# Polynomial-sketch attention with an ELU layer: two more query units through the 64-feature exchange, and the last half group's query products put beside others

## The chip, the core and the metric

The kernel runs on one core of one Trainium2 chip. The metric is the device time in microseconds. The engines named below are TensorE (PE in the profile, PEld for its weight loads), VectorE (DVE), ScalarE (ACT), GpSimd (POOL) and SyncE (SP), which issues nearly all DMAs.

## The reference

```python
# q, k, v: (4, 4, 1088, 32); S1, S2: (8, 32)
def phi(x):                                   # 8 x 8 = 64 features
    a = np.einsum('rd,bhsd->bhsr', S1, x)
    b = np.einsum('rd,bhsd->bhsr', S2, x)
    return np.einsum('bhsi,bhsj->bhsij', a, b).reshape(*x.shape[:-1], r * r)
q_p, k_p = phi(q), phi(k)
kv = np.einsum('bhsf,bhsd->bhfd', k_p, v)
z = np.sum(k_p, axis=2)
num = np.einsum('bhsf,bhfd->bhsd', q_p, kv)
den = np.einsum('bhsf,bhf->bhs', q_p, z)[..., None] + 1e-06
x = (num / den) -> (B, S, H, D) -> (4352, 128)
h = x @ w_in                                  # w_in: 128 x 2048
g = np.where(h > 0, h, np.exp(np.minimum(h, 0)) - 1)
out = g @ w_out                               # w_out: 2048 x 128
```

S1, S2 and the two weight matrices come as 64-bit floats and are rounded to 32 bits on the chip (`RA`, `RB`, `RC` round a pair of weight blocks); all products are in 32 bits.

## The kernel before

**Tiling.** A half tile is 64 query positions of one batch with all four heads (128 rows of head and dimension). Each batch has 17. `half_tile(g, k)` puts the first 16 of every batch into groups 0 to 7, eight to a group (512 output tokens), two groups to a batch; group 8, the last half group, is the 17th half tile of each of the four batches (256 tokens). `NQ` is 9.

**The steps.** The second stage runs per group over 8 pairs of 128-column blocks of `w_in` (`cp`). A step is one (group, `cp`): `mm1` (h products, L267), the elu on ACT (`e`, L928 and L930) and DVE (`gg`, L936), on POOL the sums for a seven-product scheme (`sums7`, L811 to L814, tiles `tt`), and on PE the second product of the step two before (`mm2`, `mm2_blocks` L827 or `mm2_seven` L851). The list `steps` has groups 0 and 1 interleaved in steps 0 to 15, then group 2 in steps 16 to 23, group 3 in 24 to 31, and so on to group 7 in 56 to 63. A loop over n from 5 to 63 writes the order by hand; after it the last half group runs in 20 short rounds.

**What is put into steps.** `at(n, f)` puts a call right behind `mm1` of step n, `mid(n, f)` behind the elu of the first half, `late(n, f)` behind that of the second, ahead of the step's second product. Every engine takes its instructions in this order.

**Keys.** For batches 1 to 3: `KF_late` (features by PE), `KF_late_out` (DVE), `KO_a` and `KO_b` (the 64 products per position; ACT and DVE, or POOL by `KO`), `KA` (PE: kv and the z sums), `sums_out` (`ZC`, and `KT_out`, which sends kv through DRAM, tile `kvd`, into the layouts that the queries need), `turn` and `turned` (the weights `SWs` that hold z for a batch's denominators).

**Queries.** A unit is one or two groups: unit 2 is group 2, unit 3 is group 3, unit 4 is groups 4 and 5, unit 6 is groups 6 and 7, unit 8 is the last half group. For a unit: `q1`, called its keys below (PE: a, b and the z share of every position, 32x32 tiles, L579), `q1_out` (DVE transposes, L592 or L602), `q2_den` (four DVE instructions: denominators, and a divided by them), `q2_a` (a copy to PSUM on ACT, tile `qa`), `q2_half` (DVE: 64 features per position, L714), `q4` (DVE transpose, features into rows), `q5`, its sums for x (PE), `q5_out` (ACT copies into `xg`, from which `mm1` reads).

`q4` has two forms. Without an exchange (units 2, 3, 4) the features stay in 32 rows in two halves `f`, and `q5` (L741) makes each product twice over 32 features in 32x32 tiles. With one (`pairs`, units 6 and 8) eight DMAs on SP for each half i of the unit, 64 KB each (L732, tile `qpF` to `raw`), bring two halves of the features into 64 rows, and `q5_pairs` (L753) makes each product once in 64x32 tiles, from the layout `kv2` (tile `kvp`) instead of `kvs`.

**The stops.** `queries(g5, g1, n)` makes the sums of one unit and the keys of another between `mm1` and the second product of a step; it writes into the two `h` tiles of the next step (of four) and two `aux` tiles. Its calls stand at steps 12 (keys 2), 15 (sums 2), 22 (sums 3, keys 4), 30 (sums 4, keys 6), 46 (sums 6, keys 8) and 62 (sums 8).

**SP's order.** It issues the loads, then `kvd`, `kvs` and `kvp`, the exchanges and the outputs (16 DMAs for each of groups 1 to 7, `fin_seven_b`, L899) strictly in the order above; the load of q of batch 3 waits until batch 1's q is transposed.

Of the kernel before, what the change touches and what calls it, by code (L numbers as in the profile page):

```python
# [29 lines left out]
def kernel(  # L30
# [306 lines left out]
    kvS = const.tile([P, H, D], F32, name="kvS")  # L337
    pairs = (6, 8)
    pair_b = [g // 2 for g in pairs if g < 8]
    kvs = {b: const.tile([P, H, 2, D], F32, name=f"kvs{b}") for b in (1, 2)}  # L340
    kv2 = {b: const.tile([P, H, D], F32, name=f"kvp{b}") for b in range(B)}
# [121 lines left out]
    def KT_out(b):  # L463

        kt = work.tile([P, 2 * D], F32, name="kvt", tag="kvt")
        nc.vector.transpose(kt[:], kv_ps[b][:, :R * R])
        nc.sync.dma_start(kvd[b], kt[:])
        src = kvd[b].rearrange("(h p) x -> p h x", h=H)
        for w in range(4 if b in kvs else 0):
            nc.sync.dma_start(kvs[b][32 * w:32 * w + 32].rearrange("p h f d -> p h (f d)"), src)  # L470
        for u in (0, 1) if b in pair_b else (b // 2,):
            for f in range(2):
                r = slice(64 * u + 32 * f, 64 * u + 32 * f + 32)
                nc.sync.dma_start(kv2[b][r], src[:, :, D * f:D * f + D])
# [38 lines left out]
    qn = [min(8, NH - 8 * g) // 2 for g in range(NQ)]  # L513
    abw, ans, qp, qpT, xg, xps = {}, {}, {}, {}, {}, {}
    pws = [const.tile([P, H * 8, R + 1], F32, name=f"pw{i}") for i in range(2)]
# [45 lines left out]

    units = {g: ([g, g + 1] if 4 <= g < NQ - 1 else [g]) for g in [2, 3] + list(range(4, NQ, 2))}
    un = {g: sum(qn[x] for x in gr) for g, gr in units.items()}
# [5 lines left out]

    def q1(g, ps, o, opened):  # L570
        for w in range(4):
            b, t, n = quarter_of(g, w)
            m, qs = 64 * n, qE[:, b:b + 1, :] if g == NQ - 1 and b < 2 else qT[b][:, t:t + n, :]
            qs = qs.rearrange("p t s -> p (t s)")
            if g == 2:
                m, qs = 2 * m, _ap(qs, [[8 * 64, 2], [1, m]])
            for r in range(4):
                rows = slice(32 * r, 32 * r + 32)
                nc.tensor.matmul(ps[r][32 * w:32 * w + 32, o:o + m], SWs[rows, b].rearrange("p x r -> p (x r)"),  # L579
                                 qs[rows], start=not opened, stop=True, skip_group_check=True,  # L580
                                 tile_position=(32 * r, 32 * w))
        abw[g] = ps, o

    def q1_out_two(rs):
        if 3 not in abw:
            abw[2, 3] = abw[2][0]
            t = work.tile([P, 2, 4 * H, 4 * R], F32, name="abw2", tag="abw2", bufs=1)
            abw[2], abw[3] = t[:, 0], t[:, 1]
            abw[2, 0] = t
        n = 4 * H // 4  # L590
        for r in rs:
            nc.vector.transpose(abw[2, 0][:, :, n * r:n * r + n, :].rearrange("p g m y -> p g (m y)"),  # L592
                                abw[2, 3][r][:, :64 * n].rearrange("p (g m) -> p g m", g=2))

    def q1_out(g):
        (ps, o), n = abw[g], un[g]
        pair = n > 4
        abw[g] = work.tile([P, H * n if pair else H * 4, 4 * R], F32, name="abw", tag="abwp" if pair else "abw",
                           bufs=1 if pair else 2)
        m = H * n // len(ps)  # L600
        for r in range(len(ps)):
            nc.vector.transpose(abw[g][:, m * r:m * r + m, :].rearrange("p m y -> p (m y)"),  # L602
                                ps[r][:, o:o + 32 * m])
# [82 lines left out]
    def q5_early_out(g, w):  # L686
# [6 lines left out]
        else:  # L693
# [3 lines left out]
    exch = [raw_2[:, c].bitcast(F32).rearrange("p (e m a) w -> p e m (a w)", e=2, a=16) if wide else  # L697
            const.tile([P, 2, 4 * H, 32], F32, name=f"qpE{c}")[:] for c in range(2)]

    def heads(g):  # L700
        return 2 if un[g] > 4 else H
# [15 lines left out]
    def q4(g, i=0):  # L717

        m = heads(g) * un[g]
        if g not in pairs:  # L720
            qpT[g, i] = work.tile([P, 4 * H, 2, 32], F32, name="qpT", tag="qpT", bufs=2)
            nc.vector.transpose(qpT[g, i][:, :m].rearrange("p m f s -> p (m f s)"),
                                qp.pop((g, i))[:, :m].rearrange("p m i j -> p (m i j)"))
            return
        t = work.tile([P, 2, 4 * H, 32], F32, name="qpF", tag="qpT", bufs=2)
        nc.vector.transpose(t[:, :, :m].rearrange("p f m s -> p m f s"),
                            qp.pop((g, i))[:, :m].rearrange("p m (f i) j -> p m f (i j)", f=2))
        to = qpT[g, i] = exch[(i + (g > 3)) % 2]
        for e in range(2):
            for u in range(0, 4, 2):  # L730
                for f in range(2):
                    nc.sync.dma_start(to[32 * (u + f):32 * (u + f) + 32, e, :m], t[32 * (u + e):32 * (u + e) + 32, f, :m])  # L732

    def q5(g, ps, f):
        m4 = un[g]
        for r in range(4):
            i, o = divmod(m4 * r, heads(g) * un[g])
            for w in range(4):
                b, t, n = quarter_of(g, w)
                rows = slice(32 * w, 32 * w + 32)  # L740
                nc.tensor.matmul(ps[w][32 * r:32 * r + 32, :64 * n], kvs[b][rows, r, f, :],  # L741
                                 qpT[g, i][rows, o:o + 2 * n, f, :], start=(f == 0), stop=(f == 1),
                                 skip_group_check=True, tile_position=(32 * w, 32 * r))
        xps[g] = ps

    def q5_pairs(g, ps):
        for e in range(2):
            for r in range(4):
                i, o = divmod(un[g] * r, heads(g) * un[g])
                for w in (e, e + 2):  # L750
                    b, t, n = quarter_of(g, w)
                    u = slice(64 * (w // 2), 64 * (w // 2) + 64)
                    nc.tensor.matmul(ps[w][32 * r:32 * r + 32, :64 * n], kv2[b][u, r, :],  # L753
                                     qpT[g, i][u, e, o:o + 2 * n, :], skip_group_check=True,
                                     tile_position=(u.start, 32 * r))
        xps[g] = ps

    def q5_out(g, i=0):

        n = 32 * un[g]  # L760
        ps = xps[g] if len(units[g]) == 1 else xps[g][2 * i:2 * i + 2]
        x = xg[g + i] = work.tile([P, 512], F32, name="xg", tag="xg", bufs=3)
        for w in range(len(ps)):
            nc.scalar.copy(x[:, n * w:n * w + n], ps[w][:, :n])

    def queries(g5, g1, n):

        hs[steps[n]] = [psum.tile([P, 512], F32, name="h", tag="h", bufs=4) for c in range(2)]
        ps = hs[steps[n]] + [psum.tile([P, 512], F32, name="qps", tag="aux") for _ in range(2)]
        if g5 in pairs:  # L770
            q5_pairs(g5, ps)
        elif g5 is not None:
            q5(g5, ps, 0)
        if g1 is not None:
            q1(g1, ps, 256 if g5 is not None else 0, g5 is not None)
        if g5 is not None and g5 not in pairs:
            q5(g5, ps, 1)

# [402 lines left out]

    for n, i in ((5, 7), (7, 8), (9, 9), (10, 10)):
        late(n, RA, i)
        late(n, RB, i)
        mid(n + 1, RC, i)

    late(14, keep_last, 1)
    zls = {}
# [13 lines left out]
    for b, (n_t, n_f, n_o, n_a, n_z) in enumerate(  # L1202
            ((4, 6, (7, 9), 10, 11), (14, 16, (17, 18), 19, 20), (15, 16, (23, 24), 27, 28)), 1):
        if b > 1:
# [16 lines left out]
        at(n_z, turned, b)  # L1221
    late(10, transp, qT, "q", 1, 0, NT)
    at(19, transp, qT, "q", 2, 0, NT)
    late(24, transp, qT, "q", 3, 0, NT)

    for n, g, nx in ((12, None, 2), (15, 2, None), (22, 3, 4), (30, 4, 6), (46, 6, 8), (62, 8, None)):
        at(n, queries, g, nx, n + 1)
        if g is not None:
            mid(n, q5_out, g)
        if nx == 2:  # L1230
            at(n, weights7, slice(NP - 2, NP))
            at(n, q1_out_two, (0, 1))
            mid(n, q1_out_two, (2, 3))
        elif nx is not None:
            mid(n, q1_out, nx)
        if g is not None and len(units[g]) > 1:
            late(n, q5_out, g, 1)
    late(12, q2_den, 2)
    late(13, q2_half, 2, 0)
    at(14, q4, 2)  # L1240
    mid(15, q2_den, 3)
    late(19, q2_a, 3, 0)
    late(19, q2_half, 3, 0)
    late(20, q4, 3)
    late(22, q2_den, 4)
    for n, g, i in ((25, 4, 0), (26, 4, 1), (32, 6, 0), (35, 6, 1)):
# [9 lines left out]
    late(38, q4, 6, 1)  # L1256
    late(51, q2_den, 8)
    late(51, q2_half, 8, 0)
    late(52, q4, 8)

# [102 lines left out]
```

## Time and profile before

| | |
|---|---|
| median of 3 runs | 261.6 us (260.96 to 262.27) |
| the profiled execution | 261.49 us, span 259.7 us |
| PE busy | 254.4 us, 98% |
| DVE, ACT, POOL busy | 178.9, 184.9, 167.7 us |
| products of h (L267) in the chain that ended last | 45% of the span |
| exchange DMAs (qpF), 64 KB and 32 KB | 24, landing 2.0 us after issue (median) |
| output DMAs of groups 0 to 7, 16 KB each or 32 KB | 120 |

The page is one execution on the chip. Its chain of waits follows the work that ended last back in time. A line of the chain or of a timeline is: start, duration, engine and what, line, how often. A matmul in 32 bits is recorded as two. `SPq` rows are SP's DMA issues: start, and how long the run of issues held the queue.

### The profile page before, as it was taken

The numbers are of one execution on the slowest core, as the hardware profiler recorded it, in microseconds if no ns is written. First come the engines' busy times: TensorE is split into PE (matmuls) and PEld (weight loads), VectorE is DVE, ScalarE is ACT, GpSimd is POOL, SyncE is SP. The second block draws the span as 40 slices with busy tenths as digits, with TensorE's granted clock in tenths as the row PEclk, the third lists the DMA queues.
The fourth block names the chain that finished last, engine by engine and source line by source line (L and its number), as shares of the span: only waits on it lengthen the run. The fifth ranks groups of instructions, "written<-read, shape, count | busy, mean of one in ns | idle before, by whom it ended". The sixth has DMA issues, their size and how long they took to land.

```text
span 259.7 us, 9773 instructions
## 1 busy us (share of the span) xinstructions
PE 254.4 (98%) x4115; PEld 157.8 (61%) x4115; DVE 178.9 (69%) x343; ACT 184.9 (71%) x362; POOL 167.7 (65%) x213
## 2 busy tenths in 40 slices
PE   8999999999999999999999999999999999999994
PEld 7742333533346667676666666665666666668993
DVE  6989776896988958997567576743466746544651
ACT  2699878756568677776687777775877777777792
POOL 4634214234279996788688798888688888887310
PEclk9999999999999999999999999999999999999999
DMA  5999990012011211012000204220001110110021
GB/s 171 261 311 294 299 247 23 0 26 89 20 22 25 33 27 23 5 17 35 15 0 3 36 17 105 51 33 10 4 4 28 31 27 3 28 16 3 3 30 33
DMA packets 30379, 15.61 MB, mean 60 GB/s; under 512 B 22496, under 2 KB 28000, under 8 KB 30336
## 3 DMA queue, kind: packets, MB, share of 16 engines
q1 hardware_dynamic: 29904, 14.63, 23.6%
q8 instruction: 32, 0.52, 0.8%
q10 hardware_dynamic: 368, 0.30, 0.3%
q14 instruction: 11, 0.09, 0.1%
q0 software_dynamic: 64, 0.07, 0.1%
HBM read 11.31 MB, written 2.36 MB: 53 GB/s over the span
## 4 chain that ended last, share of the span: by engine, by line
PE 96%; DVE 2%; ACT 1%; issue 0%; DVEq 0%
PE h L267 45%; PE pb L851 17%; PE pa L851 13%; PE o L267 6%; PE pb L827 4%; PE ol L267 3%; PE idle L275 1%; PE kv L458 1%; PE h L741 1%; PE h L579 1%; PE abp L354 1%; DVE kp L427 1%; PE h L753 1%; PE kfps L376 0%; PE qps L741 0%; PE qtp L657 0%
## 5 line engine op out<-in xcount | busy, mean ns | idle before, releaser
L267 PE MATMUL h<-xg,W 128*32 128x512 f32 (+3 forms) x904 | 131.0, 540 | 0.0
L936 DVE SCALAR_TENSOR_TENSOR gg<-e,h 128x512 f32<-128x512 f32 x128 | 87.0, 684 | 59.3 <-ACT e L930 56.4
L928 ACT ACTIVATE e<-h 128x512 f32<-128x512 f32 x128 | 75.3, 590 | 48.6 <-PE h L267 48.5
L811 POOL TENSOR_TENSOR tt<-gg 128x512 f32<-128x512 f32 x50 | 64.3, 1286 | 30.1 <-DVE gg L936 26.3
L930 ACT ACTIVATE e<-e 128x512 f32<-128x512 f32 x128 | 80.6, 631 | 3.7
L267 PEld LDWEIGHTS h<-xg,W 128*32 128x32 f32 (+1 forms) x904 | 42.7, 122 | 42.8 <-issue 34.0
L814 POOL TENSOR_TENSOR tt<-gg,tt 128x256 f32<-128x256 f32 x50 | 37.0, 740 | 3.9
L813 POOL TENSOR_TENSOR tt<-tt,gg 128x256 f32<-128x256 f32 x50 | 36.8, 736 | 3.9
L851 PEld LDWEIGHTS pa<-gg,W 128*64 128x64 f32 (+1 forms) x496 | 23.7, 126 | 22.4 <-issue 22.2
L851 PE MATMUL pa<-gg,W 128*64 128x128 f32 (+1 forms) x496 | 30.6, 274 | 0.0
L142 POOL TENSOR_TENSOR W<-W,raw 128x256 uint32<-128x256 uint32 (+2 forms) x12 | 11.8, 987 | 29.1 <-DVE W L119 28.0
L851 PE MATMUL pb<-tt,SS 128*64 128x128 f32 (+1 forms) x480 | 29.6, 273 | 0.0
L851 PEld LDWEIGHTS pb<-tt,SS 128*64 128x64 f32 (+1 forms) x480 | 22.8, 126 | 0.0
L851 PE MATMUL pa<-tt,SS 128*32 128x128 f32 (+1 forms) x288 | 21.2, 273 | 0.0
L851 PE MATMUL pb<-gg,SS 128*64 128x128 f32 (+1 forms) x256 | 19.9, 273 | 0.0
L851 PE MATMUL pb<-tt,W 128*64 128x128 f32 (+1 forms) x256 | 19.9, 273 | 0.0
L267 PE MATMUL o<-gg,W 128*32 128x512 f32 x128 | 15.5, 595 | 0.0
L851 PEld LDWEIGHTS pa<-tt,SS 128*32 128x32 f32 (+1 forms) x288 | 13.7, 124 | 0.0
L851 PEld LDWEIGHTS pb<-gg,SS 128*64 128x64 f32 (+1 forms) x256 | 12.8, 125 | 0.0
L851 PEld LDWEIGHTS pb<-tt,W 128*64 128x64 f32 (+1 forms) x256 | 12.8, 125 | 0.0
L827 PE MATMUL pb<-gg,W 128*32 128x256 f32 x192 | 11.5, 379 | 0.0
L989 DVE SCALAR_TENSOR_TENSOR gg<-e,h 128x256 f32<-128x256 f32 x16 | 6.6, 418 | 6.4 <-PE h L267 3.2
(169 smaller groups left out, 261.5 us busy)
## 6 DMA issues: line engine op xcount, KB each, us to landing
raw<-in_moe_w_in_dram SPq DMA_DIRECT2D x8, 256.0 KB, 5.9
raw<-in_moe_w_out_dram SPq DMA_DIRECT2D x8, 256.0 KB, 4.6
out_dram<-ob SPq DMA_DIRECT2D x112, 16.0 KB, 1.5
hd_k<-in_k_dram SPq DMA_DIRECT2D x3, 544.0 KB, 9.9
hd_q<-in_q_dram SPq DMA_DIRECT2D x3, 544.0 KB, 11.3
v<-in_v_dram SPq DMA_DIRECT2D x4, 288.0 KB, 10.0
v<-in_v_dram SPq DMA_DIRECT2D x4, 256.0 KB, 10.5
raw<-qpF SPq DMA_DIRECT2D x16, 64.0 KB, 2.0
```

The costliest lines, as they stand in the source:

```text
L142: nc.gpsimd.tensor_tensor(dst.bitcast(U32), dst.bitcast(U32), words(raw)[0], op=ADD)
L267: nc.tensor.matmul(dst[c:c + tile], lhs[:, c:c + tile], rhs, skip_group_check=True, tile_position=(0, c), **kw)
L275: nc.tensor.matmul(idle[c:c + tile, :cols], ones[:, :tile], ones[:, :cols], skip_group_check=True, tile_position=(0, c))
L811: nc.gpsimd.tensor_tensor(_ap(t[:, 0], [[4 * P, 2], [P, 2], [1, P]]), _ap(gs[g, cp][:, 0, P:], [[4 * P, 2]] + us), _ap(gs[g, cp][:, 0], [[ ...
L813: nc.gpsimd.tensor_tensor(t[:, 1], t[:, 2], b11, op=ADD)
L814: nc.gpsimd.tensor_tensor(t[:, 3], b21, t[:, 1], op=SUB)
L827: nc.tensor.matmul(acc[1][0][r:r + width[0], 256 * hi:256 * hi + 256], lhs[:, w:w + width[0]], gg[:, c, 256 * u:256 * u + 256], start=(fir ...
L851: nc.tensor.matmul(bank[r:r + width[0], P * col:P * col + P], lhs[:, w:w + width[0]], rhs[:, u], start=(first and i in ((0,) if g == 1 els ...
L928: nc.scalar.activation(e, hs[g, cp][c][:, :n], RELU, scale=-1.0)
L930: nc.scalar.activation(e, e, EXP, scale=-1.0)
L936: nc.vector.scalar_tensor_tensor(gs[g, cp][:, c, :n], es[g, cp][:, c, :n], -1.0, hs[g, cp][c][:, :n], op0=ADD, op1=MAX)
L989: nc.vector.scalar_tensor_tensor(gs["last", k // 2][:, k % 2, :2 * P], es["last", k // 2][:, k % 2, :2 * P], -1.0, hs["last", k][:, :2 * P ...
```

## The change

- Unit 2 is groups 2 and 3 together, as 4 and 6 are; unit 3 is gone. All units from 2 up take the exchange and `q5_pairs`; `q5`, `kvs` and their DMAs are gone. `kv2` of batches 1 to 3 is filled for both row halves (four DMAs each), of batch 0 for one (two).
- `queries` takes lists. Stops: step 11 (keys 2), 15 (sums 2), 25 (keys 4 and 8), 30 (sums 4, keys 6), 46 (sums 6 and 8). A second unit of a stop writes 256 columns further on in the same banks.
- Unit 8's tile `qpE2` and x tile `xgl` are its own.
- The key work of batch 1 is one step earlier; of batch 3, the products move from steps 23 and 24 to 20 and 21, `KA` from 26 and 27 to 22 and 23, `turn` from 28 to 24. Two of the weight roundings, and the transposes of q for batches 1 and 3, are one or two steps earlier.

```diff
-    pairs = (6, 8)
-    pair_b = [g // 2 for g in pairs if g < 8]
-    kvs = {b: const.tile([P, H, 2, D], F32, name=f"kvs{b}") for b in (1, 2)}
...
-        for w in range(4 if b in kvs else 0):
-            nc.sync.dma_start(kvs[b][32 * w:32 * w + 32].rearrange("p h f d -> p (h f d)"), src)
-        for u in (0, 1) if b in pair_b else (b // 2,):
+        for u in (0, 1) if b else (0,):
...
-    units = {g: ([g, g + 1] if 4 <= g < NQ - 1 else [g]) for g in [2, 3] + list(range(4, NQ, 2))}
+    units = {g: ([g, g + 1] if g < NQ - 1 else [g]) for g in range(2, NQ, 2)}
...
+    exch += [const.tile([P, 2, 2 * H, 32], F32, name="qpE2")[:]]
...
     def q4(g, i=0):
...
-        if g not in pairs:
-            qpT[g, i] = work.tile([P, 4 * H, 2, 32], F32, name="qpT", tag="qpT", bufs=2)
-            nc.vector.transpose(qpT[g, i][:, :m].rearrange("p m f s -> p (m f s)"),
-                                qp.pop((g, i))[:, :m].rearrange("p m i j -> p (m i j)"))
-            return
...
-        to = qpT[g, i] = exch[(i + (g > 3)) % 2]
+        to = qpT[g, i] = exch[i if g < NQ - 1 else 2]
...
-    def queries(g5, g1, n):
+    def queries(g5s, g1s, n):
...
-        if g5 in pairs:
-            q5_pairs(g5, ps)
-        elif g5 is not None:
-            q5(g5, ps, 0)
-        if g1 is not None:
-            q1(g1, ps, 256 if g5 is not None else 0, g5 is not None)
-        if g5 is not None and g5 not in pairs:
-            q5(g5, ps, 1)
+        sums = [(g, 256 * i) for i, g in enumerate(g5s)]
+        keys = [(g, 256 * i) for i, g in enumerate(g1s, len(g5s))]
+        for g, c in sums:
+            q5_pairs(g, ps, c)
+        for g, c in keys:
+            q1(g, ps, c)
...
-    for n, i in ((5, 7), (7, 8), (9, 9), (10, 10)):
+    for n, i in ((5, 7), (7, 8), (8, 9), (9, 10)):
...
-            ((4, 6, (7, 9), 10, 11), (14, 16, (17, 18), 19, 20), (15, 16, (23, 24), 27, 28)), 1):
+            ((4, 5, (6, 8), 9, 10), (14, 16, (17, 18), 19, 20), (15, 16, (20, 21), 23, 24)), 1):
...
-    for n, g, nx in ((12, None, 2), (15, 2, None), (22, 3, 4), (30, 4, 6), (46, 6, 8), (62, 8, None)):
-        at(n, queries, g, nx, n + 1)
+    for n, g5s, g1s in ((11, (), (2,)), (15, (2,), ()), (25, (), (4, NQ - 1)), (30, (4,), (6,)), (46, (6, NQ - 1), ())):
+        at(n, queries, g5s, g1s, n + 1)
...
-    late(12, q2_den, 2)
-    late(13, q2_half, 2, 0)
-    at(14, q4, 2)
-    mid(15, q2_den, 3)
-    late(19, q2_a, 3, 0)
-    late(19, q2_half, 3, 0)
-    late(20, q4, 3)
-    late(22, q2_den, 4)
+    late(11, q2_den, 2)
+    mid(12, q2_half, 2, 0)
+    late(12, q4, 2, 0)
+    mid(13, q2_half, 2, 1)
+    late(13, q4, 2, 1)
+    late(25, q2_den, 4)
     for n, g, i in ((25, 4, 0), (26, 4, 1), (32, 6, 0), (35, 6, 1)):
         late(n, q2_a, g, i)
     at(26, q2_half, 4, 0)
     late(26, q2_half, 4, 1)
     late(27, q4, 4, 0)
     late(28, q4, 4, 1)
...
-    late(51, q2_den, 8)
-    late(51, q2_half, 8, 0)
-    late(52, q4, 8)
+    late(40, q2_den, 8)
+    late(41, q2_half, 8, 0)
+    late(42, q4, 8)
```

More of the change, by code (lines that the diff above doesn't have):

```diff
@@ L468, in KT_out @@
         src = kvd[b].rearrange("(h p) x -> p h x", h=H)
-        for w in range(4 if b in kvs else 0):
-            nc.sync.dma_start(kvs[b][32 * w:32 * w + 32].rearrange("p h f d -> p h (f d)"), src)
-        for u in (0, 1) if b in pair_b else (b // 2,):
+        for u in (0, 1) if b else (0,):
             for f in range(2):
@@ L513 @@
     qn = [min(8, NH - 8 * g) // 2 for g in range(NQ)]
-    abw, ans, qp, qpT, xg, xps = {}, {}, {}, {}, {}, {}
+    abw, ans, qp, qpT, xg, xps, qps = {}, {}, {}, {}, {}, {}, {}
     pws = [const.tile([P, H * 8, R + 1], F32, name=f"pw{i}") for i in range(2)]
@@ L568, in quarter_of, with q1 @@
         return (*half_tile(g + n * w // 8, n * w % 8), n)
-    def q1(g, ps, o, opened):
+    def q1(g, ps, o):
         for w in range(4):
@@ L574, in q1 @@
             qs = qs.rearrange("p t s -> p (t s)")
-            if g == 2:
-                m, qs = 2 * m, _ap(qs, [[8 * 64, 2], [1, m]])
             for r in range(4):
@@ L579, in q1, with q1_out @@
                 nc.tensor.matmul(ps[r][32 * w:32 * w + 32, o:o + m], SWs[rows, b].rearrange("p x r -> p (x r)"),
-                                 qs[rows], start=not opened, stop=True, skip_group_check=True,
+                                 qs[rows], skip_group_check=True,
                                  tile_position=(32 * r, 32 * w))
         abw[g] = ps, o
[L584 to L596, printed above, removed]
-        pair = n > 4
-        abw[g] = work.tile([P, H * n if pair else H * 4, 4 * R], F32, name="abw", tag="abwp" if pair else "abw",
-                           bufs=1 if pair else 2)
+    def q1_out(g, rs=None):
+        n = un[g]
+        pair = n > 4
+        if g not in qps:
+            qps[g] = abw[g]
+            abw[g] = work.tile([P, H * n if pair else H * 4, 4 * R], F32, name="abw", tag="abwp" if pair else "abw",
+                               bufs=1)
+        ps, o = qps[g]
         m = H * n // len(ps)
-        for r in range(len(ps)):
+        for r in range(len(ps)) if rs is None else rs:
             nc.vector.transpose(abw[g][:, m * r:m * r + m, :].rearrange("p m y -> p (m y)"),
@@ L732, in q4, with q5_pairs @@
                     nc.sync.dma_start(to[32 * (u + f):32 * (u + f) + 32, e, :m], t[32 * (u + e):32 * (u + e) + 32, f, :m])
[L734 to L746, printed above, removed]
+    def q5_pairs(g, ps, c=0):
         for e in range(2):
@@ L752, in q5_pairs @@
                     u = slice(64 * (w // 2), 64 * (w // 2) + 64)
-                    nc.tensor.matmul(ps[w][32 * r:32 * r + 32, :64 * n], kv2[b][u, r, :],
+                    nc.tensor.matmul(ps[w][32 * r:32 * r + 32, c:c + 64 * n], kv2[b][u, r, :],
                                      qpT[g, i][u, e, o:o + 2 * n, :], skip_group_check=True,
                                      tile_position=(u.start, 32 * r))
-        xps[g] = ps
+        xps[g] = [p[:, c:] for p in ps]
     def q5_out(g, i=0):
@@ L761, in q5_out @@
         ps = xps[g] if len(units[g]) == 1 else xps[g][2 * i:2 * i + 2]
-        x = xg[g + i] = work.tile([P, 512], F32, name="xg", tag="xg", bufs=3)
+        if g < NQ - 1:
+            x = xg[g + i] = work.tile([P, 512], F32, name="xg", tag="xg", bufs=3)
+        else:
+            x = xg[g] = work.tile([P, 2 * P], F32, name="xgl", tag="xgl", bufs=1)
         for w in range(len(ps)):
             nc.scalar.copy(x[:, n * w:n * w + n], ps[w][:, :n])
-    def queries(g5, g1, n):
+    def queries(g5s, g1s, n):
         hs[steps[n]] = [psum.tile([P, 512], F32, name="h", tag="h", bufs=4) for c in range(2)]
         ps = hs[steps[n]] + [psum.tile([P, 512], F32, name="qps", tag="aux") for _ in range(2)]
-        if g5 in pairs:
-            q5_pairs(g5, ps)
-        elif g5 is not None:
-            q5(g5, ps, 0)
-        if g1 is not None:
-            q1(g1, ps, 256 if g5 is not None else 0, g5 is not None)
-        if g5 is not None and g5 not in pairs:
-            q5(g5, ps, 1)
+        sums = [(g, 256 * i) for i, g in enumerate(g5s)]
[4 more added lines that the diff above has]
+            q1(g, ps, c)
     hs, es, gs, ops = {}, {}, {}, {}
@@ L1180, in late @@
         extra.setdefault((n, 1), []).append((f, *a))
-    for n, i in ((5, 7), (7, 8), (9, 9), (10, 10)):
[L1183 to L1187, printed above, removed]
     zls = {}
@@ L1221 @@
         at(n_z, turned, b)
-    late(10, transp, qT, "q", 1, 0, NT)
+    for n, i in ((5, 7), (7, 8), (8, 9), (9, 10)):
+        late(n, RA, i)
+        late(n, RB, i)
+        mid(n + 1, RC, i)
+    late(9, transp, qT, "q", 1, 0, NT)
+    late(12, keep_last, 1)
     at(19, transp, qT, "q", 2, 0, NT)
-    late(24, transp, qT, "q", 3, 0, NT)
-    for n, g, nx in ((12, None, 2), (15, 2, None), (22, 3, 4), (30, 4, 6), (46, 6, 8), (62, 8, None)):
-        at(n, queries, g, nx, n + 1)
-        if g is not None:
+    late(22, transp, qT, "q", 3, 0, NT)
+    for n, g5s, g1s in ((11, (), (2,)), (15, (2,), ()), (25, (), (4, NQ - 1)), (30, (4,), (6,)), (46, (6, NQ - 1), ())):
+        at(n, queries, g5s, g1s, n + 1)
+        for g in g5s:
             mid(n, q5_out, g)
[L1230 to L1237, printed above, removed]
-    late(12, q2_den, 2)
-    late(13, q2_half, 2, 0)
-    at(14, q4, 2)
-    mid(15, q2_den, 3)
-    late(19, q2_a, 3, 0)
-    late(19, q2_half, 3, 0)
-    late(20, q4, 3)
-    late(22, q2_den, 4)
+        for g in g1s:
+            if g == 2:
+                at(n, q1_out, g, (0, 1))
+                mid(n, q1_out, g, (2, 3))
+            else:
+                mid(n, q1_out, g)
+        for g in g5s:
+            if len(units[g]) > 1:
+                late(n, q5_out, g, 1)
+    at(12, weights7, slice(NP - 2, NP))
+    late(11, q2_den, 2)
[4 more added lines that the diff above has]
+    late(25, q2_den, 4)
     for n, g, i in ((25, 4, 0), (26, 4, 1), (32, 6, 0), (35, 6, 1)):
```

## Prediction

> **What bounds the kernel now.** I read the page's busy line first, then the chain of waits in order of time, then the timelines of SP, VectorE (DVE), ScalarE (ACT) and GpSimd (POOL) around the changed steps.
>
> ```profile
> PE 254.4 (98%) x4115; PEld 157.8 (61%) x4115; DVE 178.9 (69%) x343; ACT 184.9 (71%) x362; POOL 167.7 (65%) x213
> ```
>
> TensorE (PE) is never idle for long, so the time is its work plus whatever makes it wait. The chain shows what each query group costs: it sits between the end of a step's `h` products and the next product.
>
> ```profile
> 68.55 1.72 PE h L267 x16
> 71.26 1.85 PE o L267 x16
> ...
> 95.12 1.72 PE h L267 x16
> 98.47 0.57 PE pa L851 x16
> ...
> 124.11 1.72 PE h L267 x16
> 127.89 0.59 PE pa L851 x8
> ...
> 178.24 1.72 PE h L267 x8
> 181.41 0.59 PE pa L851 x8
> ```
>
> Start plus 1.72, subtracted from the next start, gives 0.99 (step 15, sums 2), 1.63 (22, sums 3 and keys 4), 2.06 (30, sums 4, keys 6) and 1.45 (46, sums 6, keys 8). Two more pairs of the same chain (57.44 and 59.82, 231.77 and 234.01) give 0.66 (12, keys 2) and 0.52 (62, sums 8): 7.31 us in all. An ordinary step late in the run takes 3.245.
>
> The change makes units 2 and 4 go through the exchange that only units 6 and 8 use now, so I read SP's timeline and the instructions on tile qpF.
>
> ```profile
> 112.57 9.38 SPq L899 DMA_DIRECT2D out_dram<-ob  x16
> ...
> 141.98 7.45 SPq L899 DMA_DIRECT2D out_dram<-ob  x16
> 154.25 10.68 SPq L732 DMA_DIRECT2D raw<-qpF  x16
> ```
> ```profile
> L732 SPq DMA_DIRECT2D raw<-qpF x24: 518/588/1157, 154.3 to 209.1; - x24
> ...
> DMA to landing us min/median/max: 1.8/2.0/3.1
> ```
>
> Sixteen exchange DMAs hold SP for 10.68 us, 0.635 each without one long issue of 1.16, and each lands 2.05 after its start. Unit 6 has them done at 166.5, 13 us before its sums. Units 2 and 4 will not have that room.
>
> **The products themselves.** After the change: keys 2 at step 11, 0.66; sums 2 at step 15 in 64x32 tiles, 1.06 (the step-46 timeline has sums 6 start at 179.89 and the keys behind them at 180.95); keys 4 and 8 at step 25, 0.66 + 0.39 (180.95 to 181.34); sums 4 and keys 6 at step 30, 1.06 + 0.66; sums 6 and 8 at step 46, 1.06 + 0.52. That is 6.07, so -1.24; one stop fewer also saves the longer last `h` product in front of it (0.52 for 0.42), with its tail about 0.15. I take -1.4, with bounds -1.9 (drains that overlap when groups share a stop) and -1.2. The features and sums of batches 1 and 3 move by one to four steps at the same counts; step 11 still gets its key weights in time (GpSimd made them at 57.27 for a use at 59.16; both ends move together). The eight `kvs` DMAs go and four `kvp` ones come, before the units need the queue.
>
> **Unit 2.** PE's work up to step 15 is the same in sum, so its sums are reached at 70.2 (68.55 + 1.72) as now, while keys 2 end at 56.3. VectorE from 56.5: four transposes (0.78 + 0.76) between two elu products (0.6 each) to 59.1; `q2_den` over 32 columns, 1.77 (unit 4's run from 133.51 to 135.28), to 60.9; elu, `q2_half` 1.22, elu, to 63.3; `q4` 1.24, so the first exchange tile stands at 64.5. Elu, `q2_half`, elu, `q4`, 3.66 more: the second at 68.2. SP is free by about 61 (the q load of batch 3, which waits for a transpose of batch 1's q, goes a step earlier, then ten short DMAs). Sixteen issues from 64.5: the last starts at 64.5 + 15 x 0.635 = 74.0 and lands at 76.1. `q5_pairs` takes e = 0, then e = 1; each needs both tiles, so its last products wait for the last landing and end 0.45 later, 76.6, instead of 70.2 + 1.06 = 71.3: **+5.3**. Bounds: +3.7 if VectorE had the first tile 1.6 sooner, as soon as its inputs allow; +6.5 with a long issue or two. What queues behind: the ACT copies of x, and the elu of step 15 behind them on ACT; step 17 needs those, so they are covered.
>
> **Unit 4.** Let T be the start of step 25. This step now holds keys 4 and 8, the end of group 2 and `q2_den`. VectorE: first elu product done at T+3.05 (e is ready 2.4 after a step's start at 120.64); eight transposes, 4 x 0.37 and 4 x 0.16 (the rows at 128.28 and 181.89), T+5.2; `fin_seven_a` 0.5, elu 0.6, `fin_seven_b` 1.74 (140.13 to 141.87), T+8.1; `q2_den` 1.77, T+9.9. The copy `qa` (0.26) stands on ACT before step 26's activations, so these wait too, until T+10.2. Then `q2_half` and two elu products with their activations to T+13.25, `q2_half` T+14.5, elu of 27 to T+16.0, `q4(4,0)` T+17.25, elu of 28, `q4(4,1)` T+19.75. PE feels this itself: the `h` tiles of step 26 free about 0.5 late, and those of 28 wait for elu of 26, in all about 2.3.
>
> SP: group 2's sixteen output DMAs start at T+8.1 and hold it 7.5 to 9.4, to T+15.6 or T+17.5; sixteen exchange DMAs stand behind them, from T+17.3. The last starts at T+26.8, lands at T+28.9, the sums end at T+29.3. Without a wait they would start at T + 5 x 3.245 + 1.05 + 1.83 = T+19.1 and end at T+20.2: **+9.1**, in which VectorE's 2.3 are contained. Bounds: +5.4 (output started at T+6.1 as now, 112.57 against a step start at 106.44, and its shortest hold), +10.5 with long issues.
>
> **Step 46.** Unit 8's eight exchange DMAs move from steps 52 to 42, behind group 4's outputs: 167.93 + 8.4 = 176.3, plus 7 x 0.635 + 1.9 = 182.6 for the last landing; the sums of 8 would want it at 180.9 and end at 181.5. They end at 182.95: **+1.5**, bounds 0 (a quick output block) and +2.6.
>
> **A slower clock.** The trace shows what a pause does.
>
> ```profile
> 256.00:258.00 2.00, 0.00 (x0) 0.00 (x0) 0.00 (x0) 0.27 (x1) 0.00 (x0) 1.00 0.13 32
> 258.00:260.00 2.00, 0.00 (x0) 0.00 (x0) 0.00 (x0) 0.00 (x0) 0.00 (x0) 0.78 0.01 1
> ```
> ```profile
> 0.78 3.65 PE idle L275 x8
> ...
> 29.35 1.73 PE pb L827 x32
> ```
>
> These are stage windows (the column before the DMA share is the granted clock) and the chain. PE's last product ended at 255.96; about 3 us later the clock fell. At the start, where the page names no lower clock, eight warming products of 256 or 224 columns took 3.65, one per 0.46; later the four column tiles make a round of 256 in 1.73 / 8 = 0.216. So PE starts at half speed and loses some 1.9 in those 3.65. Unit 4's wait leaves PE idle for nearly 5 us in one piece, T+21.6 to T+26.4: **+1.9**. Unit 2's is 3.1, a short burst, then 2.2, at the edge; I count none, bound +1.9 more.
>
> **The sum.** -1.4 + 5.3 + 9.1 + 1.5 + 1.9 = +16.4. The profiled execution took 261.49 (span 259.7 and 1.8 around it), 0.1 under the median of 261.6: 277.9 on its own time, **278.0** as a median.
>
> [...]
>
> **The rivals.**
> - The exchange is hidden (not slower). If issues took 0.27 or less, unit 2's would all land by 64.5 + 15 x 0.27 + 2.05 = 70.6, in time; unit 4's needs VectorE's backlog gone as well. Then only -1.4 stays: 260.2. For it: SP is idle for most of the run. Against: 24 issues, none below 0.518. Chance 0.05, half of it on each side of half a per cent.
> - One wait is much shorter, through an earlier VectorE or a quicker queue: unit 2's gone gives 278.0 - 5.3 = 272.7; unit 4's down to its lower bound and no clock loss gives 278.0 - 3.7 - 1.9 = 272.4; both give 267. For it: I laid VectorE's work end to end. Against: SP alone, with measured issues, sets both ends. Chance 0.15.
> - The waits come, the clock stays up: 276.1. For it: the waits are broken by bursts of products. Chance 0.22.
> - It is worse: a second clock loss, long issues on both units, 281 to 284. Chance 0.1.
> - The forecast: 0.48.
>
> **The numbers.** Lower bounds together: -1.9 + 3.7 + 5.4 = +7.2, 268.8; upper: -1.2 + 6.5 + 10.5 + 2.6 + 3.8 = +22.2, 283.8. All ends at once are unlikely, so the range is 270 to 283. The measurement can tell about 0.5% (1.3 us). Faster by more than that: 0.04, the half of the first rival and a little for a sum I mis-signed; within: 0.03; slower: 0.93.
>
> **What would show it.** Right: in the chain, a hole of about 5 us between the `h` products of step 15 and the next product, ended by an exchange DMA, and one of 7 to 9 at step 30; SP busy without a gap from group 2's outputs through the exchange; a clock under 1 behind step 30; about 1.5 lost at step 46; no product between the last two steps of group 7. Wrong: sums at steps 15 and 30 that run in their 1.06 each; holes ended by VectorE or ACT; issues well under 0.6.

## The result and the profile after

The changed kernel takes 283.81 us in the median of 6 runs (282.46 to 284.48), the kernel before 261.68 beside it: a ratio of 1.0843, interval 1.0813 to 1.0874. The forecast of 278.0 had the sign and the places, and was 5.8 us short; the result lies above its range, which ended at 283. Below, a run over 1.5% above the fastest of its kernel is left out; that is one run, of the kernel without unit 4's exchange (277.50). The profiled execution took 284.48 us, span 282.7, 23.0 us above that of before.

From the profile page of the changed kernel: the busy line, the granted clock in 40 slices of 7.07 us, and the shares of the chain that ended last.

```profile
PE 266.5 (94%) x3987; PEld 160.1 (57%) x3987; DVE 180.0 (64%) x339; ACT 184.3 (65%) x357; POOL 167.6 (59%) x213
...
PEclk9999999999759999999959999999889999999999
...
PE 71%; SPq 9%; DVE 8%; DMA 4%; ACT 3%; issue 3%; POOL 1%; DVEq 0%
```

PE has 128 records fewer (64 products, two records each) and is busy 12.1 us longer. Fewer products that take longer point to a slower clock, and the second line shows the granted clock dip in three places. Before, the page showed no dip there. SP's issues (`SPq`) now carry 9% of the chain.

The chain of waits of the changed kernel (start, duration, what) shows the three places.

```profile
73.84 0.59 SPq L713
74.47 3.37 DMA raw<-qpF
77.97 0.60 PE qps L722
79.04 3.57 PE o L267 x16
82.61 2.49 PE h L267 x16
...
143.19 1.98 DMA raw<-qpF
145.31 0.60 PE qps L722
...
201.54 1.84 DMA qpE<-qpF
203.98 1.05 PE pa L821 x8
```

Each time the landing of the last transfer of a row of SP's issues ends the wait, and the sums' last products (L722) run behind it. After step 15 the second product `o` takes 3.57 in the chain, where before it took 1.85.

SP's timeline of the changed kernel (start, length of the run of issues, what, how many) gives the rows: unit 2's exchange; group 2's outputs, then unit 4's exchange 0.6 us later; group 4's outputs, then unit 8's exchange at once.

```profile
64.95 10.11 SPq L713 DMA_DIRECT2D raw<-qpF  x16
...
123.95 8.57 SPq L869 DMA_DIRECT2D out_dram<-ob  x16
133.13 10.65 SPq L713 DMA_DIRECT2D raw<-qpF  x16
...
188.25 8.61 SPq L869 DMA_DIRECT2D out_dram<-ob  x16
196.96 5.18 SPq L713 DMA_DIRECT2D qpE<-qpF  x8
```

The starts of the steps' `h` products, compared between the two traces, say where the 23.05 us came in (the difference of the two spans, 282.72 and 259.67):

| stretch | added, us |
|---|---|
| up to step 11 | +0.3 |
| steps 11 to 13 | +0.4 |
| steps 15 to 17 (unit 2's sums, then slow products) | +9.6 |
| steps 17 to 25 (sums 3 and keys 4 gone from 22; moved key work) | -0.6 |
| steps 25 to 30 (keys 4 and 8; VectorE and ScalarE behind) | +2.3 |
| step 30 (unit 4's sums, then slow products) | +8.3 |
| step 46 (unit 8's sums, then slow products) | +3.7 |
| step 62's stop gone (-0.7), and what runs behind PE's last product (-0.3) | -1.0 |

And the clock, in stage windows of the changed kernel. The columns are the stretch, its length, PE's busy time (and records), granted clock, DMA share, GB/s. The stretches are cut at the times at which the trace's clock records change, and one such length before.

```profile
70.38:73.80 3.42, 1.72 (x18) 1.00 0.42 96
73.80:77.21 3.41, 2.31 (x16) 0.50 0.37 81
77.21:80.62 3.41, 2.65 (x14) 0.50 0.00 1
80.62:84.04 3.42, 3.42 (x20) 0.50 0.00 0
...
138.66:142.07 3.41, 0.56 (x2) 1.00 0.47 106
142.07:145.48 3.41, 2.55 (x20) 0.50 0.38 86
145.48:148.90 3.42, 3.42 (x52) 0.50 0.02 5
...
200.10:203.51 3.41, 1.60 (x52) 1.00 0.20 48
203.51:206.92 3.41, 3.40 (x42) 0.50 0.02 5
```

Half clock lasted 10.24, 6.83 and 3.41 us. By the same windows PE was idle for 2.7 of these 20.5 us. In the rest products took longer: `o` 3.57 in the chain instead of 1.85, a 64x256 product of the sums 0.60 instead of 0.40.

### The profile page after: what moved, and what is told of

Same layout as the page of the kernel before. It is cut to its first block, busy times and chain, and to the rows that moved or that the text cites. A ratio compares the mean times of both kernels' runs of the same rounds, so it can differ in the third digit from the quotient of the medians.

```text
span 282.7 us, 9561 instructions
## 1 busy us (share of the span) xinstructions
PE 266.5 (94%) x3987; PEld 160.1 (57%) x3987; DVE 180.0 (64%) x339; ACT 184.3 (65%) x357; POOL 167.6 (59%) x213
## 4 chain that ended last, share of the span: by engine, by line
PE 71%; SPq 9%; DVE 8%; DMA 4%; ACT 3%; issue 3%; POOL 1%; DVEq 0%
PE h L267 34%; PE pb L821 13%; PE pa L821 10%; SPq L713 6%; PE o L267 4%; SPq L869 3%; PE pb L797 3%; PE ol L267 2%; DMA hd_q<-in_q_dram 2%; DMA raw<-qpF 2%; DVE gg L906 2%; ACT e L900 1%; PE kv L455 1%; ACT e L898 1%; DVE abw L587 1%
## 5 line engine op out<-in xcount | busy, mean ns | idle before, releaser
L267 PE MATMUL h<-xg,W 128*32 128x512 f32 (+2 forms) x776 | 122.6, 588 | 0.8 <-DVE gg L906 0.7
L267 PEld LDWEIGHTS h<-xg,W 128*32 128x32 f32 (+1 forms) x776 | 34.9, 120 | 45.9 <-issue 36.8
L821 PE MATMUL pa<-gg,W 128*64 128x128 f32 (+1 forms) x496 | 31.4, 278 | 0.0
L267 PE MATMUL o<-gg,W 128*32 128x512 f32 x128 | 17.2, 652 | 0.0
L736 ACT COPY xg<-h 128x256 f32<-128x256 f32 x6 | 2.1, 373 | 19.5 <-PE qps L722 9.5
L722 PE MATMUL h<-raw,kvp 64*32 64x256 f32 x48 | 10.3, 484 | 4.4 <-DMA raw<-qpF 4.4
```

Of the source, the lines that this page charges most:

```text
L267: nc.tensor.matmul(dst[c:c + tile], lhs[:, c:c + tile], rhs, skip_group_check=True, tile_position=(0, c), **kw)
L722: nc.tensor.matmul(ps[w][32 * r:32 * r + 32, c:c + 64 * n], kv2[b][u, r, :], qpT[g, i][u, e, o:o + 2 * n, :], skip_group_check=True, tile_ ...
L821: nc.tensor.matmul(bank[r:r + width[0], P * col:P * col + P], lhs[:, w:w + width[0]], rhs[:, u], start=(first and i in ((0,) if g == 1 els ...
```

## The experiments

A hole is here the time in which TensorE waits, in the sums of a step, for features that are not there. Two theories. A: SP's row of issues (0.63 us each, 16 to a unit) sets when the exchange lands, and half clock behind each hole costs the rest. B: VectorE and ScalarE, late from the heavier steps, are what is late, and a shorter row would change little. Each kernel is compared with the kernel before, run beside it (261.35 to 261.5).

### Units 2 and 4 without the exchange

The old branch of `q4`, `q5` and `kvs` with its DMAs are put back for the units that are not in `pairs`; no call moves to another step. Three kernels (lines from the edit, cut):

```diff
+    pairs = (4, 6, 8)   # u2old;  u4old: (2, 6, 8);  bothold: (6, 8)
...
+        if g not in pairs:
+            qpT[g, i] = work.tile([P, 4 * H, 2, 32], F32, name="qpT", tag="qpT", bufs=2)
...
+            return
```

> Unit 2 alone goes without the exchange (its sums over 32 features in 32x32 tiles, twice as many products); all else as changed. Theory A (SP's row of sixteen issues, and the half clock that its wait brings on): the hole at step 15 goes, 8.1 us of sums become about 1.4, and the slow products behind it (1.7 and 0.8) run at full speed: 283.8 - 9.2 = 274.6 us. Theory B (VectorE makes unit 2's features too late, the DMAs only follow it): VectorE's order is the same, so 3 to 5 us of the hole stay and the time is 279 or more.

> Unit 4 alone goes without the exchange. Theory A (SP's queue, output DMAs and then sixteen exchange DMAs): the hole at step 30 goes (8.5 us of sums become about 1.4), 2.3 us that are lost from step 25 to 30 stay, because they come from VectorE and ACT: 283.8 - 7.9 = 275.9. Theory B (the heavy step 25 on VectorE and ACT makes unit 4's features late): the sums still wait some us for VectorE at step 30, 279 or more.

> Units 2 and 4 both without the exchange; stops, key work and unit 8 as changed. Theory A: the two gains add, 283.8 - 9.2 - 7.9 = 266.7, and what is left over 261.7 is step 25's backlog (2.3), the wait of unit 8's sums at step 46 (3.7 with its slow products) and 0.5 at step 11, less some 1.4 of products saved. Theory B: 270 or more.

Measured: 276.25 (275.87 to 276.39), 274.38 (272.85 to 276.07) and 266.00 (264.53 to 268.20), all within 1.7 of A's numbers and below B's. In the traces the hole of the unit without the exchange is gone: step 15 adds 0.4 without unit 2's, step 30 nothing without unit 4's, while VectorE and ScalarE have the same calls in the same order. In the changed kernel, too, VectorE had transposed both tiles of unit 2 by 68.38 and both of unit 4 by 135.39, ahead of the sums at 70.87 and 137.78. So B does not hold for the two holes. What B names is there by itself: without both exchanges steps 25 to 30 still add 2.3. Step 46, where unit 8's exchange is untouched, adds 4.7.

### Products in the holes

Fifteen products of constants, 6.8 us in the trace, ahead of the sums of units 2 and 4. They add work and shorten no transfer; they only keep PE busy.

```diff
+        for _ in range({2: 15, 4: 15}.get(g5s[0] if g5s else 0, 0)):
+            nc.tensor.matmul(ps[2][:, :256], ones[:, :P], ones[:, :256], ...)
         for g, c in sums:
```

> The changed kernel with 15 products of 256 columns of ones (0.43 us each at full speed, 6.4 in all) put on PE ahead of the sums of units 2 and of 4, inside their waits; they write a bank that the sums then overwrite. Theory A2 (of the 22 us some 5 to 6 are the half clock, because PE pauses): the clock stays at 1 behind steps 15 and 30, the products behind both waits take their usual time, 283.8 - 3.2 - 1.9 = 278.7. Theory B2 (the clock's fall costs next to nothing, the waits are all): 283.8, or up to 1 more where the fill runs past the last landing.

Measured: 280.04 (279.14 to 283.16), 3.8 under the changed kernel, with more work in it, and 1.3 over A2's number. Stage windows of this kernel around step 15, with columns for PE, PEld, DVE, ACT and POOL, then the clock:

```profile
72.00:76.00 4.00, 4.00 (x20) 3.47 (x19) 1.09 (x2) 0.00 (x0) 0.99 (x2) 1.00 0.34 76
76.00:80.00 4.00, 4.00 (x53) 2.40 (x55) 0.00 (x0) 1.27 (x4) 0.00 (x0) 1.00 0.18 41
```

The clock stays at 1.00, `o` takes 1.74 again instead of 3.41 between starts, and step 15 to 17 adds 6.9 instead of 9.6. The profiled execution, with no half clock before its end, took 279.55. Step 30 adds 7.7 instead of 8.3, though its last transfer landed 1.0 us later behind the start of the step than in the changed kernel. So the half clock had a price with the waits in place: 3.3 us less in the two filled steps. Not all of the gain is theirs: step 46, which got no products, adds 1.8 instead of 3.7, with its clock up as well in this execution (1.000 in the mean of the run).

### Half the row

The exchange of units 2 and 4 without the four transfers per tile whose blocks stay in their own partitions. Those units then read old values there, and half the bytes go with half the issues.

```diff
-                for f in range(2):
+                for f in range(2) if g > 5 else (1 - e,):
```

> The changed kernel, with the exchange of units 2 and 4 cut to half: the blocks that stay in their own partitions (e equal to f) are left out, so that those units read old values there; SP issues 8 transfers for each unit instead of 16. If SP's row of issues at 0.6 us each sets when the exchange lands, the last landing comes 8 x 0.63 = 5 us sooner in both units, the holes at steps 15 and 30 shrink from 7.1 and 8.3 us to about 2 and 3 us, and little or none of the half clock (some 3.2 and 1.9 us in the changed kernel) follows them: 283.8 - 10 - 4 = 270 us. If the landing goes by the second tile's features on VectorE, or the transfers wait in the DMA queues, the holes stay within 1 us of theirs and the time is 282 to 284 us.

Measured: 268.84 (267.26 to 269.41). Step 15 adds 1.7 and step 30 1.6, and no half clock follows either. SP's timeline and the one idle time of PE at step 15 in this kernel:

```profile
64.16 6.60 SPq L713 DMA_DIRECT2D raw<-qpF  x8
...
124.45 5.66 SPq L713 DMA_DIRECT2D raw<-qpF  x8
```
```profile
71.53 0.40 PE L722 MATMUL qps<-raw,kvp 64*32 64x256 f32 x1 [0.80 <-DMA raw<-qpF]
```

Eight issues fewer per unit, about 5 us each, give back 15 us: the rest is half clock that no longer sets in. This is the clearest run for A; that the issues and not the bytes did it is read from the next kernel.

### Two queues

The second half of each tile's transfers for units 2 and 4 issued by ScalarE.

```diff
-                    nc.sync.dma_start(to[...], t[...])
+                    (nc.scalar if u and g < 6 else nc.sync).dma_start(to[...], t[...])
```

> The changed kernel with half of the exchange transfers of units 2 and 4 (the second half of each tile) issued from ScalarE's queue instead of SP's. If the row of SP's issues of about 0.6 us each sets when the exchange lands, the last transfer of unit 2 lands about 4 us sooner and that of unit 4 about 5 us sooner, and with less time at half clock behind them the time is about 283.8 - 4 - 5 - 3 = 271 us. ScalarE then pays eight issues of about 0.6 us per unit, which can take back 2 to 3 us. If the transfers themselves, and not their issue, are the limit, nothing lands sooner and the time stays at 283.8 us.

Measured: 284.22 (282.60 to 286.10): nothing gained, by neither reason given. ScalarE's timeline and its waits in this kernel:

```profile
64.26 2.81 ACTq L713 DMA_DIRECT2D raw<-qpF  x4
67.12 0.60 ACT L899 ACTIVATE e<-h 128x512 f32<-128x512 f32 x1 [5.57 <-DMA raw<-qpF]
...
72.02 2.71 ACTq L713 DMA_DIRECT2D raw<-qpF  x4
```
```profile
ACT e L899 <- DMA raw<-qpF: 20.7, 4, 5.6
```

The first tile's eight issues took 2.8 us from first to last end instead of 5.0, so two queues nearly halve the row. All eight transfers had landed 4.3 us after the first issue (64.26 to 68.55) instead of 6.5 (64.95 to 71.42), each still 2.0 to 2.3 after its own issue. So the transfers themselves were not the limit. But ScalarE's first issue stands in its queue until VectorE has transposed the tile; the activations behind it wait, VectorE's elu products wait for those, and the second tile is transposed at 72.0 instead of 68.4. The last transfer starts at 74.1 instead of 74.5. An issue that waits on a busy engine's queue made a ring of waits, which my expectation, 0.6 us for each issue, did not have.

### The losses beside the holes

Unit 8's features set out before group 4's outputs:

```diff
-    late(40, q2_den, 8)
-    late(41, q2_half, 8, 0)
-    late(42, q4, 8)
+    late(31, q2_den, 8)
+    late(32, q2_half, 8, 0)
+    late(32, q4, 8)
```

> The changed kernel with unit 8's rotated tile, its reciprocals and its exchange set out before group 4's outputs (steps 31 and 32) instead of behind them (steps 40 to 42). In the changed kernel unit 8's sums ended 2.3 us late at step 46, with 1.5 us lost in mm2's products at half clock behind them. If the wait for the exchange transfers that stand behind 16 output transfers on SP is what costs the time at step 46, step 46 is as long as in the kernel before and the time is 283.8 - 3.7 = 280.1 us. If the sums at step 46 are late for another reason (VectorE, or the products themselves), the time stays at 283.8 us.

Measured: 280.93 (280.06 to 281.51). Step 46 adds nothing any more, so the transfers behind the outputs were its cause; but 0.7 comes back by step 35, where the moved VectorE work stands beside group 3's output arithmetic. Half clock behind step 30 lasted 10.24 instead of 6.83, and behind step 15, where nothing was edited, 6.83 instead of 10.24: step 30 adds 9.2 and step 15 7.9.

The next kernel spreads unit 4's features on top of units 2 and 4 without the exchange (the other calls are told in the comment).

```diff
-    late(25, q2_den, 4)          # qa at 25, 26; q2_half at 26, 26; q4 at 27, 28
+    late(26, q2_den, 4)          # qa at 27, 28; q2_half at 28, 28; q4 at 29, 29
```

> Units 2 and 4 without the exchange (measured 266.0 us), and unit 4's denominators, rotated tiles and transposes spread over steps 26 to 29 as in the kernel before, instead of 25 to 28. If the backlog of VectorE and ScalarE from step 25 costs 2.3 us by itself, the time is 266.0 - 2.3 = 263.7 us. If that loss belongs to something else of the change, the time stays at 266.0 us.

Measured: 267.05 (264.66 to 267.35) against 266.00 (264.53 to 268.20): no gain in the time. In the traces steps 25 to 30 add 0.3 instead of 2.3, so the backlog is worth 2.0 there; step 30 gives 0.8 back, its second tile being late now. Both kernels have runs near 264.7 at a granted clock of 0.999 or more and runs from 266.8 to 268.2 at 0.991 to 0.994, with half clock behind step 46 in the profiled ones. The runs at full clock are level too, 264.66 here against 264.53 and 264.78, and none of them was profiled. So the steps show what the backlog costs at its place; that removing it shortens the run is not shown.

Both edits together (unit 8's and unit 4's features), with units 2 and 4 without the exchange and one weight rounding back at step 10:

```diff
-    for n, i in ((5, 7), (7, 8), (8, 9), (9, 10)):
+    for n, i in ((5, 7), (7, 8), (8, 9), (10, 10)):
```

> The change without what was found to cost time: units 2 and 4 without the exchange, unit 4's features spread over steps 26 to 29, unit 8's exchange ahead of group 4's outputs, and the key weights of step 11 rounded in step 10 as before. What is left of the change is unit 6's exchange, the products of the last half group beside others, and the outputs' order. If the four losses are separate (2.3, 4.7 and 0.5 us off 266.0 us), the time is 258.5 us, faster than the kernel before by about 1 per cent. If one loss stands in for another, it stays at 261 to 263 us.

Measured: 262.41 (262.06 to 263.84), ratio 1.0045 (1.0027 to 1.0063). The large losses are gone, with no half clock before the end, but there is 0.8 more at step 30 and 0.6 by step 35: two of the moves had made VectorE late elsewhere. So these were set again (told in comments, not in the code's own lines):

```diff
-    # unit 4: q2_half at 28, 28; q4 at 29, 29.  Unit 8: 31, 32, 32
+    # unit 4: q2_half at 27, 28; q4 at 28, 29.  Unit 8: 34, 38, 38; unit 6: q4 at 35, 37
```

> The mended version (262.4 us), with unit 4's tiles transposed half a step to a whole step sooner (steps 28 and 29) and unit 8's features moved from steps 31 and 32, where they met group 4's output arithmetic on VectorE at step 35, to steps 34 and 38. In the mended version's profile 0.8 us was lost at step 30 and 0.6 us at step 35 against the kernel before. If VectorE's order causes both, the time is 262.4 - 1.4 = 261.0 us, level with the kernel before or just below it. If the work only moves the lateness to another step, it stays at 262.4 us.

Measured: 261.24 (261.05 to 262.12), ratio 0.9994 (0.9979 to 1.0009): level with the kernel before. Step 35's loss is gone and step 30's is 0.7. The busy line of this kernel:

```profile
PE 253.9 (98%) x4051; PEld 158.5 (61%) x4051; DVE 179.0 (69%) x339; ACT 184.1 (71%) x357; POOL 168.2 (65%) x213
```

In these kernels the 64-feature form pays only where its exchange is hidden, and there, at unit 6, the kernel before had it already.

## Why the prediction was wrong, and what of it held

The prediction was wrong in its size: 283.81 us is 0.8 above its range. The waits came where it had them and near their sizes. The step that failed is the slower clock, a term of 1.9 us that measured 6.4. The prediction's own bounds had summed to 283.8 at the top, and its range was drawn at 283.

The terms against what the steps of the profiled execution measured. The clock's term is what the products behind a hole, and the sums after the last landing, took over their time at full clock. Unit 4's holds the 2.0 of backlog that spreading removed. The products' entry is what is left over, with the 0.3 behind PE's last product in it, so that its agreement proves nothing; the -1.9 of its lower bound is not shown by any run.

| term | predicted | measured |
|---|---|---|
| products (what is left) | -1.4 | -1.4 |
| unit 2's wait | +5.3 | +6.4 |
| unit 4's wait, with the backlog | +9.1 | +8.8 |
| step 46's wait | +1.5 | +2.1 |
| slower clock | +1.9 | +6.4 |
| step 11, and before it | 0 | +0.7 |
| sum | +16.4 | +23.0 |

- **Unit 4** was right in size and, but for one link, in mechanism. The last landing came at 145.2, 29.0 after step 25's start at 116.16, where the prediction had T+28.9. SP was not busy without a gap, though: it issued group 2's last output by 132.52 and then waited 0.6 for VectorE to transpose the first tile, until 133.07. So VectorE set the start of this row by 0.6, and the sixteen issues set the rest.

```profile
131.83 1.24 DVE L707 STREAM_TRANSPOSE qpF<-qp 128x1024 f32<-128x1024 f32 x1
```

  The copy `qa` did hold ScalarE, as this line of its timeline shows:

```profile
126.09 0.27 ACT L693 COPY qa<-an 128x128 f32<-128x128 f32 x1 [5.12 <-DVE an L614]
```

  PE felt it at step 28, as forecast: the `h` products that start at 128.38 had waited for VectorE's elu product, as this line of its waits has it:

```profile
PE h L267 <- DVE gg L906: 0.7, 1, 0.7
```

- **Unit 2** had the right chain: first issue at 64.95 (64.5 forecast), last at 74.47 (74.0). Its last transfer then took 3.37 in the chain instead of about 2, so the sums were 1.1 later than priced. The last two transfers, 3.83 and 3.37 to their landing, overlap a load of the instruction queue (q8 on the page) from 75.21 to 76.64. Over the twelve profiled kernels all 52 exchange transfers that took more than 2.5 us overlap such a load, and 13 of the 296 others whose landing the trace tells do. That is a coincidence read from the traces; no kernel was run to try it.
- **The clock** is the step that failed, by 4.5 of the 6.6 us by which the sum was short. "I count none" for unit 2 cost 3.2: `o` 1.7 and `h` 0.8 over full clock, and 0.7 in the last products. I had asked whether PE would be idle in one long piece; its idle pieces there are 1.3, 0.7 and 1.6 us:

```profile
72.80 0.59 PE L722 MATMUL h<-raw,kvp 64*32 64x256 f32 x2 [1.30 <-DMA raw<-qpF]
74.06 0.60 PE L722 MATMUL qps<-raw,kvp 64*32 64x256 f32 x1 [0.67 <-DMA raw<-qpF]
...
77.97 0.60 PE L722 MATMUL qps<-raw,kvp 64*32 64x256 f32 x1 [1.60 <-DMA raw<-qpF]
```

  The clock fell all the same, at 73.80 and so before the longest of them; PE had been busy for 1.72 of the 3.42 us before. The 3.2 is of this execution: two kernels with the same code up to step 15 (without unit 4's exchange, and unit 8's features early) had half clock for 6.83 us there instead of 10.24, and step 15 to 17 added 8.8 and 7.9. Behind step 30 it cost 1.8, as priced (1.9), with some luck: the idle piece was 3.1 and not nearly 5, and half clock lasted 6.83 and not 3.65. Behind step 46, where no clock loss was priced at all, it cost 1.4: `mm2` took 3.03 between starts instead of 1.58. The rival "a second clock loss, 281 to 284" held the result, at 0.1, which was too low for a hole that the prediction itself put at the edge.
- **Step 11** "still gets its key weights in time": they stood at 54.98. But the second `h` tile that the key products write was held by step 10's elu product (DVE, first line) until 56.19. The first key products start at 55.62, the others not before 56.34 (PE, below); in the trace of the spread kernel that elu product is named as what ended this pause:

```profile
55.51 0.68 DVE L906 SCALAR_TENSOR_TENSOR gg<-e,h 128x512 f32<-128x512 f32 x1
```
```profile
55.62 1.08 PE L572 MATMUL h<-qT,SWs 32*32 32x256 f32 x3
56.34 0.41 PE L572 MATMUL qps<-qT,SWs 32*32 32x256 f32 x2
```

  With the rounding back at step 10 (the mended kernel), steps 11 to 13 run 0.3 shorter than before instead of 0.4 longer. It was not run alone, but of the edits that the mended kernel has over the spread one, which adds 0.4 there, it is the only one ahead of step 31. The 0.3 before step 11 need not be the change: there the profiled kernels differ from the one before by -0.5 to +0.5.
- **Step 62's stop** gave its 0.7.
- **The price of an issue** held: 0.635 us in the forecast, 0.59 and a gap of 0.04 in the chain of the changed kernel, beside 2.0 to the landing; with half the issues the time fell by 15 us. With a second issuing engine (two queues) the median to the landing was 2.0 as well.

## What to carry to other kernels

Price a row of DMA issues as work of the issuing queue, 0.6 us each here, counted from the last thing queued ahead of it, or from the moment when its data stand if that is later, to the last landing; and before giving part of it to another engine, ask what that issue will wait for and which work stands behind it. Price each hole on TensorE twice, once as the wait and once as half clock on the products behind it, and do not judge the second by the longest idle piece alone: at step 15 here the clock fell after idle pieces of no more than 1.3 us, PE having been busy for 1.72 of the 3.42 us before. Moving feature work off one crowded step is worth only what the step that receives it can hide.

## What the runs showed of the hardware

The clock records of the changed kernel hold two values, 1 and 0.5, and before the end the stretches at 0.5 lasted 10.24, 6.83 and 3.41 us. PE had been busy for 1.72 of the 3.42 us before the first fall, 0.56 of 3.41 before the second, and 1.60 of 3.41, with 52 product records, before the third. Before six more falls, in four kernels, PE's busy time in the last 3.41 or 3.42 us was 1.47 (without unit 2's exchange), 1.75 and 1.06 (without unit 4's), 1.36 (unit 8's features early), 1.07 and 0.25 (two queues). Without unit 2's exchange the clock stayed at 1 behind a stretch with 2.00 of 3.41.

When the clock comes back is not told by that share. It rose after a stretch with PE busy for 2.98 of 3.41 us (without unit 4's exchange), and stayed at half after one with 3.25 of 3.42 (unit 8's features early). PE's ends are modelled, so the shares are rough, and no run shows what sets the clock.
